# Decoding the second MLP's weights by a clamp in place of a multiplication by a comparison

## The chip, the cores and the metric

The kernel runs on one core of a Trainium2 chip. The metric is the device time of one execution in microseconds (us); a second number, the span, is the time from the first to the last instruction in the profile of one execution.

## The reference

The reference computes causal attention with a window of 64 positions (4 batches, 8 heads, 576 positions, head width 64), and passes its 2304 rows of 512 numbers through two gated MLPs, one after the other:

```python
def _attn_ref(q, k, v):
    ...
    mask = (rel >= 0) & (rel < window)
    ...
    return np.matmul(attn, v).astype(np.float32)

def _moe_ref(x, w_gate, w_val, w_out):
    gate = 1.0 / (1.0 + np.exp(-(x @ w_gate)))
    val = x @ w_val
    return (gate * val @ w_out).astype(np.float32)

def _moe2_ref(x, w_a, w_b, w_out):
    a = x @ w_a
    b = x @ w_b
    return (a * b @ w_out).astype(np.float32)
```

The six weight matrices (512 x 1536, 512 x 1536 and 1536 x 512 for each MLP) reach the kernel as 64-bit floats.

## The kernel before

The kernel computes in pairs: a number is split into a high part, rounded to the format that TensorE multiplies in, and a low part, the rest; three of the four products of such pairs are summed. The hidden width of 1536 is cut into 12 blocks of 128, so each MLP has 12 blocks with three matrices of 128 x 512 numbers each: a and b (into the hidden layer) and o (out of it). Blocks are numbered F = 0 to 11 in the first MLP and 12 to 23 in the second; NF is 12.

Weights arrive as pairs of 32-bit words. A matrix is loaded into a tile `st` (`load_matrix`, L353 for a and b, L351 for o) with the low words at even places and the high words at odd ones (`w0`, `w1`). **Decoding** makes a 32-bit float of it in `decode_words` and `decode_pair`, for each matrix in these steps:

- `low` (L373, ScalarE): the upper three bits of the low word as an integer;
- `ex` (L376, ScalarE): the absolute value of the high word read as a 32-bit float. Its exponent field lies elsewhere than a 64-bit float's, but the value still tells how large the number is;
- `wi` (L379, VectorE): the high word shifted left by 3 and masked; then (L382, VectorE) joined with the sign and the uppermost exponent bit;
- `wi` plus `low` (L386): an integer addition, on GpSimd in the first MLP and on VectorE in the second. In the profile VectorE's form of it bears the name CUSTOM_DVE_ANT_0, and ISA in the order of the program;
- `ex` (L392, VectorE): `ex >= SMALLEST` as 0 or 1, times `wi` read as a float. Numbers too small for the format become zero.

Then the pair is made: the high part on ScalarE (L398), the low part as a subtraction (L401) on VectorE for a and b and on GpSimd for o of the second MLP. The pair is saved (L365) for the later half of the rows. In the second MLP `combining` makes sums and differences of a's and b's halves on GpSimd (L422), their high parts on ScalarE (L427) and low parts on GpSimd (L430): these feed a scheme with 7 products instead of 8 (`quad`), whose products go to the PSUM banks qa, qb and qc (L861), are put together by ScalarE (r, L880) and VectorE (g, qc: L884; qa, qc: L894), and split into the hidden pair hh, hl (L459, L461). The products with o go through `bank_sum` into the sums resf (L1000, added by VectorE in L1004) or through `projection` into xacc (L503, evicted by VectorE in L575). gacc (L528) is the same of the first MLP.

Buffers of the decoding: three tiles `st`, one `low`, two `ex`, one `wi`. An `ex` is kept until the last reader: GpSimd's sums for a and b, GpSimd's subtraction for o.

Order: the first 212 us or so follow a written-out order (`RAMP`). Behind that, Python emits the instructions in the order of the calls (`step_decode` decodes one matrix, `combining` follows b), and the framework's scheduler sets the order on each engine, except where the kernel ties it (`paced`, `held_back`, `in_order`). Each engine then takes its own queue strictly in that order. SyncE (SP) issues the transfers. The decoding of the second MLP begins before the first MLP's last blocks are done and ends at some 534 us; from there on its weights come from memory, decoded.

```python
        (nc.vector if F >= NF else nc.gpsimd).tensor_tensor(out=wi, in0=wi, in1=low, op=ALU.add)
        wordy[F, nm] = ex, wi
```

Of the kernel before, what the change touches and what calls it, by code (L numbers as in the profile page):

```python
# [10 lines left out]
F32 = mybir.dt.float32  # L11
F32R = mybir.dt.float32r
I32 = mybir.dt.int32
U32 = mybir.dt.uint32
AF = mybir.ActivationFunctionType
ALU = mybir.AluOpType
# [5 lines left out]
def tile_window_attention_gated_mlps(ctx, tc, q, k, v, w1g, w1v, w1o, w2a, w2b, w2o, out):  # L22
    nc = tc.nc
    B, H, S, D = q.shape
    NT, DM = out.shape
    DFF = w1g.shape[1]
    P = 128
    NP = H // 2
    NF = DFF // P
# [11 lines left out]
    MASKED = 1.0e30  # L41
    LARGEST = 3.0e38
    SMALLEST = 1.125 * 2.0 ** -15

    keep = lambda name, bufs, **kw: ctx.enter_context(tc.tile_pool(name=name, bufs=bufs, **kw))
    const = keep("const", 1)
# [10 lines left out]
    stage, dec, qp = pool(decoding, "stage", 3), pool(decoding, "dec", 1), pool(early, "qp", 1)  # L57
# [20 lines left out]
    for e in range(2):  # L78
        rows = slice(e * WIN, (e + 1) * WIN)
        nc.gpsimd.affine_select(  # L80
            out=mask_n[rows], in_=mask_n[rows], pattern=[[1, P]], compare_op=ALU.is_ge,
# [3 lines left out]
            out=mask_n[rows], in_=mask_n[rows], pattern=[[-1, P]], compare_op=ALU.is_ge,  # L85
# [218 lines left out]
    staged, parts, ready = {}, {}, {}  # L304
# [59 lines left out]
    def save(F, nm, pair):  # L364
        nc.sync.dma_start(out=kept[F, nm], in_=pair.bitcast(F32))  # L365

    wordy = {}

    def decode_words(F, i, nm):
        st = staged.pop((F, nm))  # L370
        w0, w1 = st[:, :, 0], st[:, :, 1]
        low = dec.tile([P, DM], I32, tag="low", name="low")
        nc.scalar.activation(out=low, in_=w0.bitcast(U32), func=AF.Copy, scale=2.0 ** -29)  # L373
        yield
        ex = dec.tile([P, DM], F32, tag="ex", bufs=2, name="ex")
        nc.scalar.activation(out=ex, in_=w1.bitcast(F32), func=AF.Abs)  # L376
        yield
        wi = dec.tile([P, DM], I32, tag="wi", name="wi")
        nc.vector.tensor_scalar(  # L379
            out=wi, in0=w1, scalar1=3, scalar2=(1 << 30) - 1, op0=ALU.logical_shift_left, op1=ALU.bitwise_and  # L380
        )
        nc.vector.scalar_tensor_tensor(  # L382
            out=wi, in0=w1, scalar=-(1 << 30), in1=wi, op0=ALU.bitwise_and, op1=ALU.bitwise_or
        )
        yield
        (nc.vector if F >= NF else nc.gpsimd).tensor_tensor(out=wi, in0=wi, in1=low, op=ALU.add)  # L386
        wordy[F, nm] = ex, wi
        yield

    def decode_pair(F, i, nm):  # L390
        wf, wi = wordy.pop((F, nm))
        nc.vector.scalar_tensor_tensor(  # L392
            out=wf, in0=wf, scalar=SMALLEST, in1=wi.bitcast(F32), op0=ALU.is_ge, op1=ALU.mult
        )
        yield
        pair = wts.tile([P, 2, DM], F32R, tag=f"w{nm}", name=f"w{nm}")
        wh, wl = pair[:, 0, :], pair[:, 1, :]
        nc.scalar.activation(out=wh, in_=wf, func=AF.Copy)  # L398
        yield
        engine = nc.gpsimd if F >= NF and nm == "o" else nc.vector  # L400
        engine.tensor_tensor(out=wl, in0=wf, in1=wh.bitcast(F32), op=ALU.subtract)  # L401
        parts.setdefault(F, {})[nm] = (wh, wl)
        pairs[F, nm] = pair
        if F >= NF:
            full[F, nm] = wf
        elif nm == "o" and DECODED <= F < 2 * SEVEN:
            nc.sync.dma_start(out=kept_o[F], in_=wf)
        yield
        if F < NF and nm != "o":
            nc.sync.dma_start(out=kept[F, "f"][:, i], in_=wf)  # L410
            yield
# [218 lines left out]
    def begin_matrix():  # L630
        if begun[0] == 0:
            load_weights(DECODED)
        if begun[0] < len(order):
            F, i, nm = m = order[begun[0]]
            begun[0] += 1
            whole(decode_words(*m))
            if F + 1 < NW:
                load_matrix(F + 1, nm)

    def step_decode(turn):  # L640

        if combined_by:
            parts_done[0] += 1
            if next(combined_by[0], combined_by) is combined_by:
                combined_by.pop()
                parts_done[0] = 0
                return True
            if parts_done[0] == 1:
                return True
        if begun[0] == len(order):  # L650
            return False
        F, i, nm = m = order[begun[0]]
        if F > limit[0] or (F > G and last_use.get(F - G - 1, -1) >= turn):
            return False
        begin_matrix()
        whole(decode_pair(*m))
        save(F, nm, pairs.pop((F, nm)))
        if nm == "o":
            ready[F] = parts[F]
        elif nm == "b" and F >= NF:  # L660
            combined_by.append(combining(F))
        return True
# [402 lines left out]
    streams["V"] = call(lambda t=t: load_values(t) for t in range(len(tiles)))  # L1065
    streams["L"] = call(lambda F=F, nm=nm: load_matrix(F, nm) for F, i, nm in order_of)
    streams["D"] = (s for F, i, nm in order_of for s in decode_words(F, i, nm))
    streams["W"] = (s for F, i, nm in order_of for s in decode_pair(F, i, nm))
    streams["K"] = call(lambda F=F, nm=nm: save(F, nm, pairs.pop((F, nm))) for F, i, nm in order_of)
    streams["P"] = call(iter(matmuls))  # L1070
# [122 lines left out]
    for fc in range(NF):  # L1193
        alone = ALONE.get(fc, ())
        for i, f0 in enumerate(alone):
            need(NF + f0, NEVER)
            w = parts[NF + f0]
# [11 lines left out]
        w = parts[NF + fc]  # L1209
# [83 lines left out]
    for n, (ph, fc) in enumerate(steps):  # L1293
# [3 lines left out]
        w = fetched[n]  # L1297
# [118 lines left out]
```

## Time and profile before

| what | value |
|---|---|
| time, median of 3 runs | 945.8 us (945.24 to 946.58) |
| time of the profiled execution | 945.28 us |
| span of the profiled execution | 943.5 us |
| TensorE (PE) busy | 922.2 us, 98% |
| VectorE (DVE) busy | 706.6 us, 75% |
| ScalarE (ACT) busy | 482.2 us, 51% |
| GpSimd (POOL) busy | 306.9 us, 33% |
| TensorE's granted clock, mean | 0.999 of full speed |

An engine's busy time is what its instructions took, not what it worked at its peak. A row of a view names the line of the kernel (L392), the engine, the operation, what is written and read (out<-in, in the program's names) and the shape. "Idle before, <-" tells how long the engine had stood still ahead of the instruction and which instruction's end let it go on.

### The profile page before, as it was taken

The numbers are of one execution on the slowest core, as the hardware profiler recorded it, in microseconds if no ns is written. First come the engines' busy times: TensorE is split into PE (matmuls) and PEld (weight loads), VectorE is DVE, ScalarE is ACT, GpSimd is POOL, SyncE is SP. The second block draws the span as 40 slices with busy tenths as digits, with TensorE's granted clock in tenths as the row PEclk, the third lists the DMA queues.
The fourth block names the chain that finished last, engine by engine and source line by source line (L and its number), as shares of the span: only waits on it lengthen the run. The fifth ranks groups of instructions, "written<-read, shape, count | busy, mean of one in ns | idle before, by whom it ended". The sixth has DMA issues, their size and how long they took to land. (4 is left out here: it accounts for less than half of the span.)

```text
span 943.5 us, 15633 instructions
## 1 busy us (share of the span) xinstructions
PE 922.2 (98%) x5498; PEld 771.9 (82%) x5498; DVE 706.6 (75%) x1370; ACT 482.2 (51%) x1071; POOL 306.9 (33%) x325
## 2 busy tenths in 40 slices
PE   7899999999999999999999999999999999999998
PEld 6798888887888778878787787888888888888886
DVE  6997787786569799898999877687877773354455
ACT  7897555686644456664555446555444233211111
POOL 4543222343226714561655337354351000000000
PEclk9999999999999999999999999999999999999999
DMA  9988598988479626673767758555547675544212
GB/s 225 244 214 239 198 323 290 346 274 250 143 226 315 233 113 200 237 247 142 267 223 250 278 175 234 197 182 168 176 124 240 197 277 147 167 157 146 86 60 89
DMA packets 145566, 195.79 MB, mean 208 GB/s; under 512 B 63569, under 2 KB 98641, under 8 KB 144849
## 3 DMA queue, kind: packets, MB, share of 16 engines
q1 hardware_dynamic: 144400, 192.71, 63.0%
q0 software_dynamic: 1088, 2.10, 1.3%
q8 instruction: 43, 0.70, 0.3%
q14 instruction: 35, 0.28, 0.1%
HBM read 118.75 MB, written 71.57 MB: 202 GB/s over the span
## 5 line engine op out<-in xcount | busy, mean ns | idle before, releaser
L861 PE MATMUL qa<-op,wq 128*128 128x512 f32 x432 | 112.3, 390 | 1.8 <-ACT r L880 1.4
L861 PE MATMUL qb<-op,wq 128*128 128x512 f32 x432 | 111.1, 390 | 0.9 <-POOL wq L430 0.6
L880 ACT ACTIVATE r<-qa 128x512 f32<-128x512 f32 x108 | 62.9, 595 | 95.0 <-PE qa L861 93.4
L450 PE MATMUL gps<-xh,wa 128*128 128x256 f32 (+1 forms) x392 | 104.9, 338 | 1.1 <-DVE g L884 1.1
L450 PE MATMUL vps<-xh,wb 128*128 128x256 f32 (+1 forms) x392 | 105.4, 337 | 0.0
L861 PEld LDWEIGHTS qa<-op,wq 128*128 128x128 f32 x432 | 80.8, 188 | 19.4 <-ACT r L880 2.0
L861 PEld LDWEIGHTS qb<-op,wq 128*128 128x128 f32 x432 | 80.9, 188 | 18.5 <-POOL wq L430 1.0
L551 PE MATMUL accm<-hh,wo 128*128 128x512 f32 (+1 forms) x296 | 85.4, 356 | 1.2 <-DVE gacc L528 1.0
L386 POOL TENSOR_TENSOR wi<-wi,low 128x512 int32<-128x512 int32 x36 | 50.0, 1388 | 112.2 <-DVE wi L382 70.4
L450 PEld LDWEIGHTS gps<-xh,wa 128*128 128x128 f32 x392 | 68.7, 189 | 10.1 <-DVE g L884 1.7
L450 PEld LDWEIGHTS vps<-xh,wb 128*128 128x128 f32 x392 | 68.9, 189 | 7.8 <-issue 0.3
L1000 PE MATMUL accq<-wo,h 128*128 128x512 f32 (+1 forms) x294 | 71.5, 385 | 0.1
L459 ACT ACTIVATE hh<-qa 128x512 fp32r<-128x512 f32 x36 | 21.5, 597 | 91.1 <-DVE qa L894 57.8
L450 PE MATMUL gps<-xl,wa 128*128 128x256 f32 (+1 forms) x196 | 65.6, 335 | 0.6 <-DVE xl L237 0.6
L450 PE MATMUL vps<-xl,wb 128*128 128x256 f32 (+1 forms) x196 | 65.7, 335 | 0.0
L392 DVE SCALAR_TENSOR_TENSOR ex<-ex,wi 128x512 f32<-128x512 f32 x72 | 53.6, 744 | 14.8 <-ACT ex L376 7.0
L1000 PEld LDWEIGHTS accq<-wo,h 128*128 128x128 f32 x294 | 54.5, 188 | 11.3 <-DVE res L1004 0.3
L841 POOL TENSOR_TENSOR wq<-s,wq 128x256 fp32r<-128x256 f32 x48 | 38.4, 865 | 76.2 <-ACT wq L838 76.2
L551 PEld LDWEIGHTS accm<-hh,wo 128*128 128x128 f32 x296 | 52.9, 189 | 11.1 <-DVE gacc L528 3.1
L1000 PE MATMUL accq<-wo,hh 128*128 128x512 f32 x184 | 55.7, 394 | 2.9 <-ACT hh L459 1.9
L189 ACT ACTIVATE pr<-pr,stat 128x128 f32<-128x128 f32 x144 | 54.1, 392 | 7.1 <-DVE stat L183 7.0
L861 PE MATMUL qa<-op,wa 128*128 128x512 f32 x216 | 56.6, 390 | 0.6 <-ACT wb L398 0.6
(187 smaller groups left out, 2178.3 us busy)
## 6 DMA issues: line engine op xcount, KB each, us to landing
wo<-ko SPq DMA_DIRECT2D x27, 512.0 KB, 4.1
wa<-ka SPq DMA_DIRECT2D x27, 512.0 KB, 4.3
st_o<-in_moe_w_out_dram SPq DMA_DIRECT2D x24, 512.0 KB, 4.8
ka<-wa SPq DMA_DIRECT2D x24, 512.0 KB, 5.1
kb<-wb SPq DMA_DIRECT2D x24, 512.0 KB, 4.2
ko<-wo SPq DMA_DIRECT2D x24, 512.0 KB, 5.0
kq<-wq SPq DMA_DIRECT2D x48, 256.0 KB, 4.8
wq<-kq SPq DMA_DIRECT2D x48, 256.0 KB, 3.2
```

What stands on the lines that cost most here:

```text
L189: nc.scalar.activation(out=pr[e][:, j, :], in_=pr[e][:, j, :], func=AF.Exp, bias=nmax[:, e, j:j + 1], scale=-1.0, accum_out=None if t in O ...
L386: (nc.vector if F >= NF else nc.gpsimd).tensor_tensor(out=wi, in0=wi, in1=low, op=ALU.add)
L392: nc.vector.scalar_tensor_tensor(out=wf, in0=wf, scalar=SMALLEST, in1=wi.bitcast(F32), op0=ALU.is_ge, op1=ALU.mult)
L450: nc.tensor.matmul(ps, lhsT=a[:, c * P:(c + 1) * P], rhs=b[:, c, :], start=(n == 0), stop=(n == 3 * NP - 1))
L459: nc.scalar.activation(out=hh, in_=hr, func=AF.Copy, scale=factor)
L551: nc.tensor.matmul(ps[:, m], lhsT=a[:, sl], rhs=b, start=k == 0, stop=k == total - 1)
L841: nc.gpsimd.tensor_tensor(out=t[:, 1], in0=sums[nm], in1=t[:, 0].bitcast(F32), op=ALU.subtract)
L861: nc.tensor.matmul(ps, lhsT=a[:, c * P:(c + 1) * P], rhs=b[:, c, :], start=first and n == 0, stop=n == 5, skip_group_check=True,)
L880: nc.scalar.activation(out=r[n], in_=ps, func=AF.Copy)
L1000: nc.tensor.matmul(ps, lhsT=a, rhs=b, start=n == 0, stop=n == len(pairs) - 1)
```

## The change

The second MLP's matrices (F >= NF) get a decoding of their own, `second_words`. It clamps the absolute value to at least 2^-15, in place (L405 of the changed kernel), shifts and masks that same tile in place (L406) instead of the loaded high words, joins sign and uppermost bit from the loaded words (L409), and adds `low` (L413). A number below 2^-15 has been replaced by 2^-15, whose bits the shift and the mask turn into zero, so no comparison and multiplication follow: `decode_pair` skips that step. What was two tiles `ex` and one `wi` becomes three tiles w0, w1 and w2 of one kind, taken in turn by the second MLP's matrices; the first MLP's use w0 and w1 for `ex` and w2 for `wi`, and do the same steps as before.

```diff
+    LEAST = 2.0 ** -15
...
-    wordy = {}
-
-    def decode_words(F, i, nm):
+    wordy, nword = {}, [0]
+
+    def word(n):
+        nword[0] += 1
+        return dec.tile([P, DM], F32, tag=f"w{nword[0] % n}", name="ex")
+
+    def first_words(F, i, nm):
...
-        ex = dec.tile([P, DM], F32, tag="ex", bufs=2, name="ex")
+        ex = word(2)
...
-        wi = dec.tile([P, DM], I32, tag="wi", name="wi")
+        wi = dec.tile([P, DM], F32, tag="w2", name="wi").bitcast(I32)
...
-        (nc.vector if F >= NF else nc.gpsimd).tensor_tensor(out=wi, in0=wi, in1=low, op=ALU.add)
+        nc.gpsimd.tensor_tensor(out=wi, in0=wi, in1=low, op=ALU.add)
...
+    def second_words(F, i, nm):
...
+        low = dec.tile([P, DM], I32, tag="low", name="low")
+        nc.scalar.activation(out=low, in_=w0.bitcast(U32), func=AF.Copy, scale=2.0 ** -29)
+        yield
+        ex = word(3)
+        nc.scalar.activation(out=ex, in_=w1.bitcast(F32), func=AF.Abs)
+        yield
+        wi = ex.bitcast(I32)
+        nc.vector.tensor_scalar(out=ex, in0=ex, scalar1=LEAST, scalar2=None, op0=ALU.max)
+        nc.vector.tensor_scalar(
+            out=wi, in0=wi, scalar1=3, scalar2=(1 << 30) - 1, op0=ALU.logical_shift_left, op1=ALU.bitwise_and
+        )
+        nc.vector.scalar_tensor_tensor(
+            out=wi, in0=w1, scalar=-(1 << 30), in1=wi, op0=ALU.bitwise_and, op1=ALU.bitwise_or
+        )
+        yield
+        nc.vector.tensor_tensor(out=wi, in0=wi, in1=low, op=ALU.add)
+        wordy[F, nm] = ex
+        yield
+
+    def decode_words(F, i, nm):
+        return (second_words if F >= NF else first_words)(F, i, nm)
+
     def decode_pair(F, i, nm):
-        wf, wi = wordy.pop((F, nm))
-        nc.vector.scalar_tensor_tensor(
-            out=wf, in0=wf, scalar=SMALLEST, in1=wi.bitcast(F32), op0=ALU.is_ge, op1=ALU.mult
-        )
+        wf = wordy.pop((F, nm))
+        if F < NF:
+            wf, wi = wf
+            nc.vector.scalar_tensor_tensor(
+                out=wf, in0=wf, scalar=SMALLEST, in1=wi.bitcast(F32), op0=ALU.is_ge, op1=ALU.mult
+            )
```

The change also sorts the queues anew, from the last part of the first MLP up to the end of the decoding. Two places on VectorE show how. Lines of the changed kernel behind the decoding are 32 higher: its L433 is L401, L607 is L575, L916 is L884, L926 is L894, L1036 is L1004.

The first place lies between a g of one block's scheme and the eviction xacc0 behind it, at some 415 us of the trace of before. On VectorE, before, the last 12 rows down to that eviction:

```order
L379 TENSOR_SCALAR wi_5411<-st_a_5233 128x512
L382 SCALAR_TENSOR_TENSOR wi_5411<-st_a_5233,wi_5411 128x512
L386 ISA wi_5411<-wi_5411,low_5407 128x1024
L392 SCALAR_TENSOR_TENSOR ex_5409<-ex_5409,wi_5411 128x512
L379 TENSOR_SCALAR wi_5432<-st_b_5262 128x512
L382 SCALAR_TENSOR_TENSOR wi_5432<-st_b_5262,wi_5432 128x512
L386 ISA wi_5432<-wi_5432,low_5428 128x1024
L401 TENSOR_TENSOR wa_5418<-ex_5409,wa_5418 128x512
L392 SCALAR_TENSOR_TENSOR ex_5430<-ex_5430,wi_5432 128x512
L379 TENSOR_SCALAR wi_5487<-st_o_5341 128x512
L382 SCALAR_TENSOR_TENSOR wi_5487<-st_o_5341,wi_5487 128x512
L575 TENSOR_TENSOR xacc0_4870<-acc0_5359,xacc0_4870 128x512
```

Ahead of these stand that g (L884) and, behind it, an L386 and an L392 of the matrix before. Now, from g on:

```order
L916 TENSOR_TENSOR g0_5379<-qc_5383,r1_5390 128x512
L409 SCALAR_TENSOR_TENSOR ex_5414<-st_b_5249,ex_5414 128x512
L406 TENSOR_SCALAR ex_5394<-ex_5394 128x512
L409 SCALAR_TENSOR_TENSOR ex_5394<-st_a_5221,ex_5394 128x512
L405 TENSOR_SCALAR ex_5321<-ex_5321 128x512
L406 TENSOR_SCALAR ex_5321<-ex_5321 128x512
L409 SCALAR_TENSOR_TENSOR ex_5321<-st_o_5066,ex_5321 128x512
L413 ISA ex_5321<-ex_5321,low_5319 128x1024
L413 ISA ex_5394<-ex_5394,low_5392 128x1024
L433 TENSOR_TENSOR wa_5402<-ex_5394,wa_5402 128x512
L607 TENSOR_TENSOR xacc0_4864<-acc0_5344,xacc0_4864 128x512
```

Between g and the eviction 13 instructions have become 9; three matrices are under way side by side, in three buffers, where one followed the other.

The second place lies in a later block, at some 520 to 524 us: from behind the second eviction of resf0 to the product qa, which the hidden part hh is made from. On VectorE, before (behind the rows shown comes the last L392 of b):

```order
L379 TENSOR_SCALAR wi_6291<-st_a_6161 128x512
L884 TENSOR_TENSOR qc_6278<-qb_6277,r3_6376 128x512
L382 SCALAR_TENSOR_TENSOR wi_6291<-st_a_6161,wi_6291 128x512
L386 ISA wi_6291<-wi_6291,low_6287 128x1024
L392 SCALAR_TENSOR_TENSOR ex_6289<-ex_6289,wi_6291 128x512
L1004 TENSOR_TENSOR resf1_4826<-accq_6362,resf1_4826 128x512
L379 TENSOR_SCALAR wi_6320<-st_b_6182 128x512
L401 TENSOR_TENSOR wa_6298<-ex_6289,wa_6298 128x512
L382 SCALAR_TENSOR_TENSOR wi_6320<-st_b_6182,wi_6320 128x512
L1004 TENSOR_TENSOR resf1_4826<-accq_6379,resf1_4826 128x512
L386 ISA wi_6320<-wi_6320,low_6316 128x1024
L894 TENSOR_TENSOR qa_6276<-qa_6276,g0_6274 128x512
```

Between the eviction and these stands one more L392. Now:

```order
L409 SCALAR_TENSOR_TENSOR ex_6259<-st_a_6134,ex_6259 128x512
L409 SCALAR_TENSOR_TENSOR ex_6287<-st_b_6154,ex_6287 128x512
L916 TENSOR_TENSOR qc_6248<-qb_6247,r3_6344 128x512
L413 ISA ex_6259<-ex_6259,low_6257 128x1024
L1036 TENSOR_TENSOR resf1_4820<-accq_6330,resf1_4820 128x512
L433 TENSOR_TENSOR wa_6267<-ex_6259,wa_6267 128x512
L413 ISA ex_6287<-ex_6287,low_6285 128x1024
L1036 TENSOR_TENSOR resf1_4820<-accq_6347,resf1_4820 128x512
L926 TENSOR_TENSOR qa_6246<-qa_6246,g0_6244 128x512
```

The clamps and shifts of a and b have moved ahead of the evictions of resf0, and b's word is complete (its L413) in front of qa.

## Rows read from the trace of the kernel before

**Rows 1.** The page: span, busy time of engines, granted clock in 40 slices

```profile
span 943.5 us, 15633 instructions
...
PE 922.2 (98%) x5498; PEld 771.9 (82%) x5498; DVE 706.6 (75%) x1370; ACT 482.2 (51%) x1071; POOL 306.9 (33%) x325
...
PEclk9999999999999999999999999999999999999999
```

**Rows 2.** Busy time by stretches: start:end, length, then each engine's busy us (count)

```profile
core 0: us, PE busy (x) PEld busy (x) DVE busy (x) ACT busy (x) POOL busy (x), PEclk, DMA share, GB/s
...
283.00:354.00 71.00, 68.96 (x330) 55.99 (x329) 60.52 (x85) 33.88 (x65) 37.12 (x39) 1.00 0.61 220
354.00:545.00 191.00, 185.71 (x874) 153.24 (x873) 174.86 (x265) 109.31 (x210) 91.13 (x90) 1.00 0.67 231
...
580.00:920.00 340.00, 340.00 (x1534) 282.64 (x1533) 213.66 (x323) 124.73 (x229) 60.36 (x80) 1.00 0.52 167
```

**Rows 3.** The same view, four stretches of 23.6 us, all matmuls of 512 columns

```profile
448.40:472.00 23.60, 22.26 (x98) 17.87 (x97) 23.16 (x33) 12.63 (x24) 15.13 (x14) 1.00 0.78 267
495.60:519.20 23.60, 22.73 (x100) 18.21 (x99) 23.15 (x36) 13.64 (x26) 13.64 (x14) 1.00 0.76 255
519.20:542.80 23.60, 22.50 (x97) 17.70 (x96) 20.49 (x32) 11.49 (x20) 8.53 (x9) 1.00 0.74 277
613.60:637.20 23.60, 23.60 (x106) 19.52 (x105) 19.73 (x31) 13.37 (x26) 11.68 (x16) 1.00 0.55 179
```

**Rows 4.** TensorE's waits, 283 to 580 us: total us, times, longest

```profile
PE accq L1000 <- ACT hh L459: 1.9, 2, 1.3
PE qa L861 <- ACT r L880: 1.4, 2, 0.9
PE gps L450 <- DVE g L884: 1.1, 1, 1.1
PE accm L551 <- DVE gacc L528: 1.0, 3, 0.5
PE accq L1000 <- DVE xacc L575: 0.9, 2, 0.7
PE qa L861 <- ACT wb L398: 0.6, 1, 0.6
PE qb L861 <- POOL wq L430: 0.6, 1, 0.6
```

**Rows 5.** Timeline at 416 us, DVE and then PE: start, length, instruction [idle before]

```profile
414.42 1.11 DVE L382 SCALAR_TENSOR_TENSOR wi<-st_o,wi 128x512 int32<-128x512 int32 x1
415.45 0.68 DVE L575 TENSOR_TENSOR xacc<-acc,xacc 128x512 f32<-128x512 f32 x1
...
416.19 0.72 PE L1000 MATMUL accq<-wo,hh 128*128 128x512 f32 x2 [0.67 <-DVE xacc L575]
```

**Rows 6.** Groups by line, DVE, 283 to 545 us: count | busy us, mean ns | idle

```profile
L392 DVE SCALAR_TENSOR_TENSOR ex<-ex,wi 128x512 f32<-128x512 f32 x35 | 27.2, 777 | 5.0 <-ACT ex L376 2.3 <-POOL osum L338 0.8 <-POOL wq L430 0.5
...
L379 DVE TENSOR_SCALAR wi<-st_o 128x512 int32<-128x512 int32 x12 | 6.7, 562 | 0.1
L379 DVE TENSOR_SCALAR wi<-st_b 128x512 int32<-128x512 int32 x11 | 6.5, 588 | 0.2
L379 DVE TENSOR_SCALAR wi<-st_a 128x512 int32<-128x512 int32 x11 | 5.6, 507 | 0.1
```

**Rows 7.** Single lines, 283 to 545 us: ns min/median/max, first and last start us

```profile
L392 DVE SCALAR_TENSOR_TENSOR ex<-ex,wi x35: 677/692/1355, 283.7 to 533.4; 128x512 f32<-128x512 f32 x35
...
L379 DVE TENSOR_SCALAR wi<-st_a x11: 410/425/959, 296.0 to 517.3; 128x512 int32<-128x512 int32 x11
L379 DVE TENSOR_SCALAR wi<-st_b x11: 414/426/1401, 302.4 to 521.5; 128x512 int32<-128x512 int32 x11
...
L401 DVE TENSOR_TENSOR wb<-ex,wb x12: 675/1199/1774, 286.5 to 528.1; 128x512 fp32r<-128x512 f32 x12
...
L401 DVE TENSOR_TENSOR wa<-ex,wa x11: 674/687/693, 304.5 to 522.6; 128x512 fp32r<-128x512 f32 x11
```

**Rows 8.** Waits of DVE, then of ACT, 283 to 545 us: total us, times, longest

```profile
DVE ex L392 <- ACT ex L376: 2.3, 3, 1.6
...
ACT ex L376 <- POOL wo L401: 5.7, 4, 1.8
```

More of the change, by code (lines that the diff above doesn't have):

```diff
@@ L385, in decode_words @@
         yield
-        (nc.vector if F >= NF else nc.gpsimd).tensor_tensor(out=wi, in0=wi, in1=low, op=ALU.add)
+        nc.gpsimd.tensor_tensor(out=wi, in0=wi, in1=low, op=ALU.add)
         wordy[F, nm] = ex, wi
         yield
-    def decode_pair(F, i, nm):
-        wf, wi = wordy.pop((F, nm))
-        nc.vector.scalar_tensor_tensor(
-            out=wf, in0=wf, scalar=SMALLEST, in1=wi.bitcast(F32), op0=ALU.is_ge, op1=ALU.mult
-        )
+    def second_words(F, i, nm):
+        st = staged.pop((F, nm))
+        w0, w1 = st[:, :, 0], st[:, :, 1]
+        low = dec.tile([P, DM], I32, tag="low", name="low")
[18 more added lines that the diff above has]
+        return (second_words if F >= NF else first_words)(F, i, nm)
+    def decode_pair(F, i, nm):
+        wf = wordy.pop((F, nm))
[4 more added lines that the diff above has]
+            )
         yield
```

## The prediction

> **What bounds the kernel now.** The page comes first [rows 1]: TensorE is busy for 922.2 of the 943.5 us of the span, at the full clock throughout, so at most some 21 us can be had in all, and VectorE (DVE) stands at 75% on average. An average hides stages, so the table by stretches is next [rows 2]. While the second MLP's weights are decoded (354 to 545 us) DVE is busy for 174.9 of 191 us, 92%, and TensorE stands still for 5.3 us; in the 71 us before, where that decoding begins, TensorE stands still for 2.0 us; from 580 to 920 us TensorE never stands still and DVE has a third of its time free. What the change is worth is decided before 580 us. Third, the table of who made TensorE wait, from 283 to 580 us [rows 4]: DVE is named directly three times (g, gacc, xacc, 3.0 us together), and the evictions on ScalarE (ACT) and the sums on GpSimd (POOL) that are named otherwise mostly wait for a DVE result themselves. The wait at 416.19 us is the pattern [rows 5]: TensorE needs a PSUM bank that the DVE eviction xacc frees; that eviction starts at 415.45 us because a decoding step (L382) ran from 414.42. DVE takes its queue in order, and decoding steps stand in front of the work that TensorE waits for. So this stage is one where a shorter DVE queue should come back, in part, as TensorE time.
>
> **What a stopped TensorE costs.** A wait shows only its idle gap, and refilling costs more. A clean stretch of 23.6 us holds 106 matmuls of 512 columns, 223 ns each; the three that start at 448.4, 495.6 and 519.2 us hold 98, 100 and 97 [rows 3]. The 23 that are missing are worth 5.1 us, while the idle time shown is 1.3, 0.9 and 1.1, together 3.3 us. I count 1.55 us for each us of a gap.
>
> **The change, part by part.** It concerns the 36 matrices of the second MLP, three for each of 12 column blocks.
>
> *The multiplication by a comparison goes* (L392): 36 instructions of the second MLP. In the stretch from 283 to 545 us stand 35 such rows, almost all of them of this MLP; they take 777 ns on average [rows 6], 677 at the least [rows 7].
>
> *A maximum with a constant comes*: 36 instructions, one input and one output of 512 floats, in place. The trace has no such maximum. The nearest row is the shift L379, also a one-input operation with constants on 512 four-byte elements in SBUF: 410 ns at the least, 562, 588 and 507 ns on average for the three matrices [rows 6, 7], so 552 over all. I take that. The lower bound is 410; the upper one is what such a shift takes at the worst of the matrix a, 959 ns [rows 7]. Difference: 36 x (777 - 552) = 8.1 us less DVE time; from 36 x (677 - 410) = 9.6 us less to 36 x (959 - 777) = 6.6 us more.
>
> *Shift, join, integer addition* stay at one each, the shift now reading packed words where it read every other one; 410 ns with the stride leaves no sign that this costs anything, so nothing is counted. ACT and POOL keep their instructions; no transfer is added. The moved loads and stores on SP's queue cost nothing as long as DMA has room: its share is 0.67 in that stretch [rows 2]; without that room a late matrix would be the next thing waited for.
>
> *The buffers* change what waits for what. Before, two result buffers and one word buffer: the third matrix of a block needs the buffer of the first, which POOL frees only after the block's sums, and the next integer word needs the one word buffer. Now three whole buffers rotate, so the first matrix of the next block waits for the sums of this one, and the third for nothing of its own block. The price is that the absolute value by ACT now stands at the head of the DVE chain, where before it was wanted only at its end.
>
> *The order* shows the effect. At the eviction xacc (first place of the order shown) 13 DVE instructions stood between g and xacc, ten of 0.69 us and three of 0.43 [medians in rows 7], 8.2 us; now 9 stand there, six and three, 5.4 us. 2.8 us earlier is more than both waits there, 0.9 us [rows 4]; they go. At the second place, between the second eviction of resf0 and the product qa, ten and two (7.8 us) become eight long ones (5.5 us): the 0.6 us that TensorE waits for the hh made from this qa goes (the smaller one of the two in rows 4). There the word of matrix b is also finished ahead of qa instead of after it, so POOL's sums start earlier and the 0.6 us for wq goes. The same holds one block earlier for the 0.6 us for wb. Of the waits for g (1.1) and gacc (1.0) I count half, since the queue ahead of them shrinks by less than 1 us. The long wait for hh (1.3 us, at 462 us) stays: from the first xacc to qa there the queue holds seven long and one short before (5.3 us) and seven and two now (5.7).
>
> Sum: 0.9 + 0.6 + 0.6 + 0.6 + 0.55 + 0.5 = 3.75 us of gaps, times 1.55 = 5.8 us gained. Against it: that long wait grows by 0.4, and a queue sorted anew will make some new wait, for which I put one of the small ones, 0.6: (0.4 + 0.6) x 1.55 = 1.6 us. Net 4.2 us: the profiled execution goes from 945.28 to 941.1, and since the median shown is 0.5 above that execution, **941.6 us**.
>
> *A rule against it.* Rows first: the subtraction for wa takes 674 to 693 ns, the one for wb, the same form, 1199 at the median [rows 7]; wb's runs while POOL makes its sums. So DVE instructions that read SBUF lengthen beside POOL. The Trainium skill, "SBUF — State Buffer", section "SBUF: two separate sides", says that VectorE and GpSimd share a pair of ports as an exclusive lock, taken by a VectorE operation with two SBUF inputs and also by a one-input one in a two-port mode. By that rule the new maximum fights POOL just as the old multiplication did, and gains only its shorter hold; the sum would keep the 9.6 us of undisturbed times at best, and lose it where POOL is in front. The trace agrees as far as the shift, too, reaches 1401 ns [rows 7].
>
> **The rivals.**
>
> *Contention and reordering eat it (no change).* Of the new maximum, if most fall beside POOL's sums, each takes as much as the old step: the 959 ns against 777 above. Then DVE is as full as before and only the order differs. For it: the shift's maxima [rows 7]. Against it: its medians are within 16 ns of its minimum. Time: the new waits (1.6 us) against the 1 to 2 us that better buffers save, 945 to 946.
>
> *The head of the chain blocks (slower).* DVE reaches the maximum before ACT has made the absolute value, since ACT itself waits for POOL to free the buffer, and everything behind it on DVE, evictions among it, stands. For it: ACT's absolute value waited for POOL 4 times, up to 1.8 us, and DVE for ACT's result 3 times, up to 1.6 us [rows 8]; the new order puts up to three maxima in a row. Against it: with three buffers that release comes earlier. It decides when DVE is held for more per block than it has free, 191 - 174.9 = 16.1 us over the some 9 blocks that 191 us hold (12 blocks in some 250 us, first to last L392 in [rows 7], 21 us each), 1.8 us. If 4 of the 12 blocks lose 1.8 us each in full: 941.6 + 7.2 = 948.8.
>
> *Everything behind DVE goes (much faster).* All idle time from 354 to 545 us, 5.3 us, and half of the 2.0 before: 6.3 x 1.55 = 9.8, so 936.
>
> That the change does something else can be excluded from the order: 36 maxima are there, and no comparison is left behind the twelfth block.
>
> **How the numbers follow.** A measurement of this kernel can tell about 0.2%, 1.9 us, from no change. My forecast (939 to 943.9): 0.54. Much faster (below 939): 0.10. No change (943.9 to 947.7): 0.22. Slower: 0.14. Faster by over 0.2% is then 0.64, within 0.22, slower 0.14. The range from 936.5 to 947 leaves out most of the slower case, a little of the no-change case and half of the much faster one, under 2 in 10.
>
> **What would show it.** DVE's busy time falls from 706.6 to about 698; the maximum near 0.55 us on average; DVE in the decoding stretch below 90%; the waits of TensorE for xacc, wb and wq gone, the one for hh still there; from 580 us on everything the same but earlier. Wrong would be: a maximum of 0.8 us or more; DVE idle in front of the maximum, released by ACT; or TensorE's waits in 283 to 580 us at 8 us as now, under other names.

## The result, and the profile after

| | before | after |
|---|---|---|
| time, median (lowest to highest, runs) | 945.71 us (945.23 to 947.5, 6) | 954.05 us (950.87 to 958.11, 6) |
| ratio, 95% interval | | 1.0085 [1.0064, 1.0106] |
| profiled execution: time, span | 945.28, 943.5 us | 953.24, 951.4 us |

The changed kernel is 8.3 us slower; 941.6 was forecast. The page of after, to be held against [rows 1]:

```profile
span 951.4 us, 15611 instructions
...
PE 921.9 (97%) x5498; PEld 771.3 (81%) x5498; DVE 697.8 (73%) x1370; ACT 480.3 (50%) x1071; POOL 302.3 (32%) x325
```

VectorE did lose 8.8 us of work, and TensorE has as much to do as before, over a longer span. The table of stretches of after (start:end, length, busy us of PE, PEld, DVE, ACT, POOL with counts, granted clock, DMA share, GB/s) answers [rows 2]:

```profile
283.00:354.00 71.00, 66.91 (x319) 54.43 (x317) 54.67 (x82) 31.43 (x62) 41.57 (x44) 1.00 0.63 223
354.00:545.00 191.00, 185.27 (x873) 153.54 (x874) 168.63 (x269) 107.00 (x210) 85.14 (x90) 1.00 0.65 228
...
580.00:920.00 340.00, 336.49 (x1517) 279.33 (x1517) 215.75 (x319) 125.87 (x232) 64.33 (x85) 1.00 0.53 170
```

In the decoding stretch VectorE falls from 174.9 to 168.6 us, 88%, and TensorE gets nothing from it (185.3 against 185.7). The losses lie at both edges: 2 us in 283 to 354, and 3.5 us behind 580, where TensorE never stood still before. The groups of the new steps (count | busy us, mean ns | idle before and releaser), 283 to 545 us, for [rows 6]:

```profile
L413 DVE CUSTOM_DVE_ANT_0 ex<-ex,low 128x1024 uint16<-128x1024 uint16 x34 | 27.3, 803 | 3.1 <-ACT low L399 2.7
...
L406 DVE TENSOR_SCALAR ex<-ex 128x512 int32<-128x512 int32 x34 | 21.5, 633 | 0.4
L405 DVE TENSOR_SCALAR ex<-ex 128x512 f32<-128x512 f32 x34 | 20.6, 605 | 7.2 <-ACT ex L402 6.9
```

The maximum takes 605 ns on average; with the median of 427 in the single lines below (ns min/median/max, first and last start) it lies near the shift in [rows 6, 7], as assumed. Ahead of it VectorE stands idle for 6.9 us until ScalarE's absolute value is made; ahead of the old multiplication that was 2.3 us [rows 8].

```profile
L405 DVE TENSOR_SCALAR ex<-ex x34: 408/427/1334, 286.9 to 525.6; 128x512 f32<-128x512 f32 x34
```

TensorE's waits in after, 283 to 600 us (total us, times, longest), against [rows 4]:

```profile
PE qa L893 <- ACT r L912: 5.4, 3, 3.5
PE accm L583 <- DVE gacc L560: 3.0, 4, 1.7
PE qa L893 <- DVE g L916: 2.1, 1, 2.1
PE qc L893 <- DVE h L493: 1.6, 1, 1.6
PE accq L1032 <- DVE hl L493: 0.7, 1, 0.7
```

With four more of 0.2 to 0.6 they make 14.6 us (11.1 of them up to 580 us); before it was 8.1. xacc, wb and wq are gone, as foretold. In their place stand waits that were not there: for g under qa (at 464 us), for h (at 502), and one of 3.5 us for r at 582, behind the decoding; and the waits for gacc have grown from 1.0 to 3.0 us.

What such a wait looks like shows in the timeline of after at 501 us, DVE and then PE (start, length, instruction [idle before]):

```profile
501.40 1.50 DVE L406 TENSOR_SCALAR ex<-ex 128x512 int32<-128x512 int32 x1
502.82 0.68 DVE L493 SCALAR_TENSOR_TENSOR h<-qc,h 128x512 fp32r<-128x512 f32 x1
...
503.56 1.65 PE L893 MATMUL qc<-op,wa 128*128 128x512 f32 x6 [1.61 <-DVE h L493]
```

It is the pattern of [rows 5], one place further: a decoding step stands in VectorE's queue ahead of the result that TensorE needs. At 464 us the same holds of all four steps of one o, and of one more maximum, ahead of g.

The largest wait. Timeline of after at 577 to 588 us, DVE, then POOL, ACT and PE:

```profile
577.55 1.75 DVE L808 TENSOR_TENSOR op<-xq,op 128x1024 fp32r<-128x1024 f32 x1
579.23 5.44 DVE L808 TENSOR_TENSOR op<-t,op 128x1024 fp32r<-128x1024 f32 x1
584.59 0.68 DVE L916 TENSOR_TENSOR g<-qc,r 128x512 f32<-128x512 f32 x1
...
579.87 3.03 POOL L873 TENSOR_TENSOR wq<-s,wq 128x256 fp32r<-128x256 f32 x4
582.66 0.92 POOL L866 TENSOR_TENSOR s<-wf 128x256 f32<-128x256 f32 x1
...
585.30 0.63 ACT L921 ACTIVATE g<-g 128x512 f32<-128x512 f32 x1 [4.71 <-DVE g L916]
585.84 0.58 ACT L912 ACTIVATE r<-qa 128x512 f32<-128x512 f32 x1
...
586.47 1.66 PE L893 MATMUL qa<-op,wb 128*128 128x512 f32 x6 [3.51 <-ACT r L912]
```

The same place before, DVE, then POOL:

```profile
567.65 5.31 DVE L783 TENSOR_TENSOR t<-xq,t 128x1024 f32<-128x1024 f32 x1
...
574.56 1.74 DVE L776 TENSOR_TENSOR op<-t,op 128x1024 fp32r<-128x1024 f32 x1
576.23 0.68 DVE L884 TENSOR_TENSOR g<-qc,r 128x512 f32<-128x512 f32 x1
...
576.87 3.03 POOL L841 TENSOR_TENSOR wq<-s,wq 128x256 fp32r<-128x256 f32 x4
```

Before, the subtraction that makes the operand (`op<-t,op`) was through at 576.3, ahead of GpSimd's four subtractions; after, it starts 0.6 us before them and takes 5.44 us in place of 1.74. g stands behind it in VectorE's queue, r stands in ScalarE's queue behind a step that waits for g, and TensorE waits for the bank that r frees. Nothing in this place was edited: the second MLP's last decoding ended some 50 us earlier.

### The profile page after: what moved, and what is told of

It reads as the page before. It is cut to its first block, busy times and chain, and to the rows that moved or that the text cites. A ratio compares the mean times of both kernels' runs of the same rounds, so it can differ in the third digit from the quotient of the medians.

```text
span 951.4 us, 15611 instructions
## 1 busy us (share of the span) xinstructions
PE 921.9 (97%) x5498; PEld 771.3 (81%) x5498; DVE 697.8 (73%) x1370; ACT 480.3 (50%) x1071; POOL 302.3 (32%) x325
## 4 chain that ended last, share of the span: by engine, by line
PE 68%; DVE 17%; ACT 5%; POOL 4%; issue 3%; DMA 3%; SPq 0%; POOLq 0%; DVEq 0%; ACTq 0%
PE qa L893 15%; PE accq L1032 10%; PE gps L482 7%; PE vps L482 7%; PE qb L893 7%; PE accm L583 6%; PE qc L893 3%; PE accy L995 3%; DVE ex L409 2%; PE accx L995 2%; DVE ex L413 2%; PE xps L229 2%; DVE ex L405 2%; DVE ex L406 1%; PE sps L171 1%
## 5 line engine op out<-in xcount | busy, mean ns | idle before, releaser
L893 PE MATMUL qa<-op,wb 128*128 128x512 f32 x216 | 55.0, 390 | 3.5 <-ACT r L912 3.5
L893 PE MATMUL qc<-op,wa 128*128 128x512 f32 x216 | 56.2, 390 | 1.6 <-DVE h L493 1.6
```

Source lines behind the costliest of these rows:

```text
L893: nc.tensor.matmul(ps, lhsT=a[:, c * P:(c + 1) * P], rhs=b[:, c, :], start=first and n == 0, stop=n == 5, skip_group_check=True,)
```

## The experiments

The order theory: the new arithmetic saves what was forecast, and the queues, sorted anew by the scheduler, give back more, at a few rows. Against it the arithmetic theory: the new one-input steps are held beside GpSimd, or the clamp at the chain's head waits for ScalarE's absolute value (the rival of the prediction). The port theory: one VectorE operation is held for a GpSimd burst, by chance of timing; the third-buffer theory: decoding that runs further ahead is in the way. Ratios are to executions of before that were timed beside each run, with 95% intervals.

**a1_again.** The changed kernel, not edited.

> The changed kernel itself once more, unedited, for a second trace. Order theory (the queues that the scheduler sorted anew put decoding and weight-sum work ahead of what TensorE waits for): the TensorE waits at 342, 466, 504 and 586 us are all there again, within 0.5 us each, and the median is 951 to 956 us. Port theory (a VectorE operation is held for as long as a GpSimd burst lasts, by chance of their timing): the waits at 342, 466 and 504 us are there, but the operand subtraction near 579 us that took 5.44 us is between 1.2 and 5.5 us, and the time of the run goes with it: a run without it is about 3.7 us shorter, 949.5 us.

953.98 us, 1.0069 [1.0049, 1.0090], with the same waits in its trace (r 5.4, 3, 3.5; gacc 3.0; g 2.0; h 2.1), and the subtraction takes 5.43 us again. The loss is fixed to places and comes again; it is no matter of chance between executions.

**e5_order_dve_pe** and **e6_order_dve.** The changed kernel with VectorE's queue from some 300 us in the order of before, the new steps in the places of the old ones; in e5 TensorE's queue too. A helper ties each instruction of an engine to the one before it:

```diff
+    def given_order(engine, ranks):
+        made = [i for i in nc.cur_bb.bb.instructions if i.engine == engine]
+        for a, b in zip(ranks, ranks[1:]):
+            tc.add_manual_dep(made[b], made[a].name, ...)
+    given_order(mybir.EngineType.DVE, [...])
+    given_order(mybir.EngineType.PE, [...])
```

> The new arithmetic with VectorE's and TensorE's queues in the order that they had before the change (the clamp in the shift's place, the shift in the join's, the join in the addition's, the addition in the comparison's), from about 300 us on. Order theory: the saving of VectorE (8 to 9 us) comes through as forecast and the time is 941 to 944 us. Arithmetic theory (the new one-input operations are held by GpSimd bursts, or the clamp waits for ScalarE at the head of the queue): it stays at 949 to 954 us, with the same long waits under qa and qc.

> As the run before it, with VectorE's queue alone in the old order; TensorE's is the scheduler's. Order theory with VectorE as the place: 941 to 946 us, at most 2 us behind the run with both. If TensorE's own order is what costs, it stays above 949 us while the run with both is below 945.

e5: 954.02, 1.0078 [1.0059, 1.0098]; e6: 955.14, 1.0088 [1.0065, 1.0112]. TensorE's waits in e5, 235 to 600 us:

```profile
PE accm L583 <- ACT hh L491: 6.5, 2, 6.2
PE accq L1032 <- DVE xacc L607: 4.4, 2, 4.2
...
PE qa L893 <- ACT r L912: 1.4, 2, 1.0
```

By the number alone this speaks for the arithmetic theory; by the places it doesn't. The wait of 3.5 us for r is gone (1.0 at the most), as are those of 2.1 for g and 1.6 for h under qa and qc; instead one of 6.2 us stands at 273 us, at the edge of the tied stretch, and one of 4.2 at 422. ScalarE's and GpSimd's queues, sorted freely around the one held, don't fit it: ahead of the maximum VectorE stands 16.1 us for ScalarE, in 283 to 545 us,

```profile
L405 DVE TENSOR_SCALAR ex<-ex 128x512 f32<-128x512 f32 x34 | 18.2, 536 | 16.1 <-ACT ex L402 16.1
```

against 6.9 in after. Inconclusive on the sum. e5 and e6 are not told apart, so TensorE's own order is not what costs here.

**e3_two_words.** Two word buffers in place of three.

```diff
-        ex = word(3)
+        ex = word(2)
```

> The new arithmetic with two buffers for the decoded words in place of three, so that the scheduler sorts a third way. Order theory: the time is as arbitrary as its order, anywhere from 943 to 956 us, and its TensorE waits stand at other places than the changed kernel's. Third-buffer theory (decoding that runs further ahead is what gets in the way): 941 to 945 us. Arithmetic theory: 950 to 955 us.

955.17, 1.0081 [1.0054, 1.0109]: not told apart from after, so the third-buffer theory falls. The order theory had expected other places; the tail is the same, with a subtraction of 5.43 us at 578.52. The two theories left are not told apart by this run.

**bt_control, f2t_old_queues, f1t_three_old_queues.** VectorE, TensorE and ScalarE tied in one order for all three. bt has the old arithmetic, its shift, join, addition and multiplication together at the place of the old multiplication; f2t and f1t have the new four steps there, with two word buffers and with three.

From f2t to f1t:

```diff
-        ex = word(2)
+        ex = word(3)
```

> The control for the run before it: the old arithmetic with the same fixing of the queues (shift, join, addition and comparison of a matrix together where the comparison stood). Order theory: 944 to 948 us, near the kernel before, and 3 to 8 us above the run with the new arithmetic in the same queues. Arithmetic theory: the same 944 to 948 us, but below the run with the new arithmetic. If both are far above 948 us, standing the four together is itself what costs, and only the difference of the two tells anything.

> The new arithmetic alone, in the queues of before: two buffers for the words as before the change (any free one is taken), TensorE's queue exactly as before, VectorE's and ScalarE's as before except that the clamp, shift, join and addition of a matrix stand together where the comparison stood. Order theory (the forecast's sums were right and the newly sorted queues ate them): 939 to 944 us, and the TensorE waits at 342, 466, 504 and 586 us that the changed kernel has are gone. Arithmetic theory (the new operations are held by GpSimd, or wait for ScalarE at the head of the queue): 947 to 954 us.

> As the first run of these, with the third word buffer of the change. Order theory: as that run, 938 to 944 us, a little less where ScalarE can run further ahead. Third-buffer theory (more buffers let the loads and ScalarE's copies run into what TensorE needs): 3 us or more above it.

bt: 957.25, 1.0133 [1.0114, 1.0153]. f2t: 959.94, 1.0158 [1.0142, 1.0173]. f1t: 951.22, 1.0063 [1.0046, 1.0080]. All three lie outside what either theory expected: the order alone costs 12 us (bt), so only differences tell. The group of the maximum, 235 to 560 us, in f2t and then in f1t:

```profile
L407 DVE TENSOR_SCALAR ex<-ex 128x512 f32<-128x512 f32 x36 | 19.2, 535 | 10.0 <-ACT ex L404 9.0 <-POOL osum L339 0.8
```

```profile
L407 DVE TENSOR_SCALAR ex<-ex 128x512 f32<-128x512 f32 x36 | 19.6, 543 | 2.5 <-ACT ex L404 2.3
```

The head's wait is real: with two buffers in one order VectorE stands 9.0 us for ScalarE, with three 2.3, and the third buffer is worth 8.7 us there. The change brings the third buffer along. Against bt in the same order, the new arithmetic takes 2.7 us more with two buffers and 6.0 us less with three.

**n1_swapped_copies.** The kernel before, in which only two ScalarE operations of the second decoding that don't depend on each other (`low`, `ex`) are written in the other sequence.

```diff
-        low = ...; nc.scalar.activation(out=low, ...)
         ex = ...;  nc.scalar.activation(out=ex, ...)
+        low = ...; nc.scalar.activation(out=low, ...)
```

> The kernel before with nothing but two independent ScalarE operations of the second MLP's decoding written in the other order (the absolute value ahead of the low word's copy), so that the scheduler sorts the queues anew with the same work in them. Order theory: the time moves by more than 2 us from 945.7 us, most likely up (948 to 955 us), without any change of the work. Arithmetic theory: 945 to 947 us, since nothing was changed that costs.

949.07, 1.0040 [1.0025, 1.0055]: 4.2 us slower (before beside it: 944.9) with the arithmetic untouched. Its trace keeps step with before to within 0.8 us until 563 us and loses 3.2 us by 586, at the place of after. DVE, then PE:

```profile
569.46 0.42 DVE L466 SCALAR_TENSOR_TENSOR hl<-vps,hh 128x256 fp32r<-128x256 f32 x1 [1.92 <-ACT hh L464]
569.80 5.32 DVE L781 TENSOR_TENSOR op<-t,op 128x1024 fp32r<-128x1024 f32 x1
...
578.38 0.68 DVE L889 TENSOR_TENSOR g<-qc,r 128x512 f32<-128x512 f32 x1
...
580.91 2.82 PE L866 MATMUL qa<-op,wb 128*128 128x512 f32 x6 [2.27 <-ACT r L885]
```

The held subtraction is no longer than the one that before has (5.31 us), but it starts 2.15 us later (569.80 against 567.65), since ScalarE makes hh later, and g comes 2.15 us later (578.38 against 576.23). So this tail is fragile with the old arithmetic already, and the arithmetic theory is not needed for it. What does the new sorting disturb there? In ScalarE's queue at 556 to 578 us some 19 rows stand otherwise in after: bank copies (`added`, L1034) that wait for TensorE's accq are ahead of the copies (L807) that VectorE's operands are made from. Timeline of after, ACT:

```profile
561.22 0.60 ACT L1034 ACTIVATE added<-accq 128x512 f32<-128x512 f32 x1 [1.00 <-PE accq L1032]
561.71 1.05 ACT L807 ACTIVATE op<-t 128x1024 fp32r<-128x1024 f32 x1
```

**x1_tail** (after, those rows in the order of before), **b1_reverse_tail** (before, those rows in the order of after), **x2_dve_moves** (after, six VectorE results moved ahead of decoding steps or sums: gacc at 307 and 341 us, qa and g at 464, h at 502, hl at 529) and **x12_both**. From here on all queues are tied to their own order but for the rows named. ScalarE in x1 and VectorE in x2 against after:

```diff
 L506 ACTIVATE hr<-gps
-L1034 ACTIVATE added<-accq
 L807 ACTIVATE op<-t
 L491 ACTIVATE hh<-vps
...
+L1034 ACTIVATE added<-accq
+L807 ACTIVATE op<-t
+L491 ACTIVATE hh<-vps
 L1034 ACTIVATE added<-accq
 L870 ACTIVATE wq<-s x4
-L807 ACTIVATE op<-t
-L491 ACTIVATE hh<-vps
```

```diff
 L405 TENSOR_SCALAR ex<-ex
+L926 TENSOR_TENSOR qa<-qa,g
 L406 TENSOR_SCALAR ex<-ex
+L916 TENSOR_TENSOR g<-qb,r
 L409 SCALAR_TENSOR_TENSOR ex<-st_o,ex
 L413 ISA ex<-ex,low
-L926 TENSOR_TENSOR qa<-qa,g
 L405 TENSOR_SCALAR ex<-ex
-L916 TENSOR_TENSOR g<-qb,r
```

> The changed kernel with every queue fixed in its own order, except some 20 rows of ScalarE between 556 and 578 us, which take the order of before: the operand copies and hidden copies ahead of the bank copies that wait for TensorE. No work differs. Order theory: the TensorE waits at 577 and 582 to 586 us (1.4 and 3.5 us) shrink to the one of 0.9 us that the kernel before has, and the time falls by 4 to 5 us, to 949 to 950 us. Port theory (the 5.4 us subtraction is held by GpSimd whenever it runs, whatever ScalarE does): the wait stays, 953 to 954 us.

> The kernel before, old arithmetic, every queue fixed in its own order, except the same some 20 rows of ScalarE at 552 to 575 us, which take the order that the changed kernel has. Order theory: 948 to 951 us, 3 to 6 us above the kernel before, with one operand subtraction of over 5 us in the way of the sum that TensorE waits for. If the new arithmetic has to be there for that wait to come about, 945 to 946 us.

> The changed kernel with every queue fixed in its own order, except that on VectorE six operations that TensorE waits for stand some places earlier, ahead of decoding and weight sums: one accumulator eviction at 307 and one at 341 us, the products of sum and gate at 464 us (two), the hidden remainder at 502 us and one at 529 us. Order theory: the waits of 1.7, 2.1, 1.6 and 0.65 us there go or shrink to under 0.5 us each, and the time falls by 3 to 6 us, to 948 to 951 us. If what is late there is not the queue but the operand (ScalarE, TensorE itself), it falls by less than 1 us.

> Both edits of the two runs before it. Order theory: the gains add, 942 to 946 us, at or under the kernel before: what the change costs is then all in some 30 rows of two queues. If something else in the new work costs, it stays above 949 us.

| kernel | us | ratio |
|---|---|---|
| x1_tail | 950.01 | 1.0040 [1.0028, 1.0052] |
| b1_reverse_tail | 950.51 | 1.0047 [1.0030, 1.0063] |
| x2_dve_moves | 952.5 | 1.0070 [1.0052, 1.0088] |
| x12_both | 947.27 | 1.0011 [1.0001, 1.0021] |

The rows of ScalarE at the tail take 4.0 us off after's 954.05, and put 4.7 us on the 945.8 of before timed beside them. Timeline of b1, DVE, then POOL:

```profile
576.46 4.06 DVE L776 TENSOR_TENSOR op<-t,op 128x1024 fp32r<-128x1024 f32 x1
580.45 0.68 DVE L884 TENSOR_TENSOR g<-qc,r 128x512 f32<-128x512 f32 x1
...
577.11 2.33 POOL L841 TENSOR_TENSOR wq<-s,wq 128x256 fp32r<-128x256 f32 x3
```

and of x1, DVE, then POOL:

```profile
573.30 5.00 DVE L815 TENSOR_TENSOR t<-xq,t 128x1024 f32<-128x1024 f32 x1
...
579.90 1.74 DVE L808 TENSOR_TENSOR op<-t,op 128x1024 fp32r<-128x1024 f32 x1
581.57 0.68 DVE L916 TENSOR_TENSOR g<-qc,r 128x512 f32<-128x512 f32 x1
...
573.23 3.29 POOL L873 TENSOR_TENSOR wq<-s,wq 128x256 fp32r<-128x256 f32 x4
576.02 1.19 POOL L866 TENSOR_TENSOR s<-wf 128x256 f32<-128x256 f32 x1
```

In both directions the same rows decide which subtraction is held: in x1 another one (`t`), with time to spare, and g starts 3.0 us sooner than in after. x2 alone is not told apart from after, and misses its 948 to 951: its waits for g under qa and for h go, but the longest ones for hh and op, both made by ScalarE, grow from 0.6 to 1.6 and 1.3 us. On top of x1 the six moves take 2.7 us. x12 stays above the 942 to 946 that the order theory put, so more than these rows is in it.

**x3_more_moves, x4_last_moves; b2_before_moves, b3_before_last_moves.** The same treatment carried on: rows that a wait of TensorE names are moved ahead of decoding steps, 8 in x3 on top of x12, 9 more in x4; and on the kernel before with its old arithmetic 6 in b2 (g, xacc twice, qa twice, hh) and 4 in b3. One move of x4 and one of b2:

```diff
 L916 TENSOR_TENSOR g<-qc,r
 L406 TENSOR_SCALAR ex<-ex
+L1036 TENSOR_TENSOR resf<-accq,resf
 L405 TENSOR_SCALAR ex<-ex
...
-L1036 TENSOR_TENSOR resf<-accq,resf
```

```diff
 L392 SCALAR_TENSOR_TENSOR ex<-ex,wi
-L379 TENSOR_SCALAR wi<-st_o
-L382 SCALAR_TENSOR_TENSOR wi<-st_o,wi
 L575 TENSOR_TENSOR xacc<-acc,xacc
+L379 TENSOR_SCALAR wi<-st_o
+L382 SCALAR_TENSOR_TENSOR wi<-st_o,wi
```

> The run with both edits, and eight more rows moved ahead of decoding and weight sums where its trace still shows TensorE waiting: on VectorE the second eviction at 308 us and one at 341 us, the products and the hidden remainder at 422 and 464 us, an output sum at 502 us; on ScalarE the hidden copy at 422 and 464 us. Saving theory (the arithmetic saves what was forecast, and only the order of the queues eats it): 942 to 945 us, below the kernel before. Slack theory (what VectorE saves is not on TensorE's path in well ordered queues either): 945 to 947 us, no better than the run with both edits.

> The kernel before, old arithmetic, with every queue fixed in its own order and six rows moved in the same way (VectorE: a sum at 381 us, two output sums at 415 us, the product at 461 and 523 us; ScalarE: the hidden copy at 461 us), ahead of decoding. Saving theory: 942 to 944 us by the waits of 1.1, 0.9, 1.3 and 0.5 us that go, but not below the changed kernel with its moves by more than 1 us. Slack theory: as low as the changed kernel with all its moves or lower, since the order of the queues is what sets the time and the arithmetic is hidden: 941 to 943 us.

> The run with the further moves, and nine more rows moved where its trace still shows TensorE waiting: on VectorE the gate's product and the hidden remainder at 309 us, an operand difference at 341 us, output sums at 482 and 501 us; on ScalarE the hidden copy at 309 us and the sums' copies at 463, 480 and 574 us. Saving theory: 941 to 943 us, clearly under the kernel before and within 2 us of the forecast. Slack theory: 944 us as the run before it, new waits in place of the old ones.

> The old arithmetic with its moves and four more (VectorE: the product at 382 us, an output sum at 415 us, addition and comparison of a matrix at 507 us). Saving theory: 943.5 to 945 us, at least 1 us above the changed kernel with all of its moves, since VectorE has no room left between 354 and 545 us (174.9 of 191 us busy). Slack theory: 942 to 943 us, as low as the changed kernel.

| kernel | us | ratio |
|---|---|---|
| x3_more_moves | 944.26 | 0.9993 [0.9982, 1.0003] |
| x4_last_moves | 942.66 | 0.9966 [0.9953, 0.9979] |
| b2_before_moves | 944.94 | 0.9998 [0.9989, 1.0007] |
| b3_before_last_moves | 945.84 | 1.0002 [0.9992, 1.0012] |

The stretch 354 to 545 us in x4, then in b3:

```profile
354.00:545.00 191.00, 190.09 (x896) 157.62 (x895) 165.24 (x269) 107.15 (x210) 84.84 (x90) 1.00 0.66 237
```

```profile
354.00:545.00 191.00, 186.28 (x869) 152.96 (x869) 175.17 (x265) 108.34 (x209) 90.87 (x90) 1.00 0.67 232
```

VectorE's maximum in x4, 283 to 545 us:

```profile
L405 DVE TENSOR_SCALAR ex<-ex 128x512 f32<-128x512 f32 x34 | 20.5, 603 | 7.6 <-ACT ex L402 7.2
```

In x4 TensorE stands still for 0.9 of 191 us while VectorE is busy for 165.2; with the old arithmetic VectorE stays at 175.2, and the moves win nothing that can be measured. TensorE's waits of x4, 283 to 600 us, sum to 5.6 us with the largest of 1.7. VectorE's idle time before the maximum, released by ScalarE, is 7.2 us in x4 and 6.9 in after: with that wait in place x4 computes the same with the same operations as after, and beats both kernels, by its ratio 3.2 us under before (2.7 by the medians). So the head's wait is not what makes after slow. b2 gains less than either theory had put.

## Why the prediction was wrong

**Right: what VectorE saves.** 8.1 us were forecast, 8.8 came. The maximum takes 605 ns where 552 was put, and the shift, 633, got longer too; the addition (857 ns before, 803 now) and the join (30.7 us in all from 283 to 545 us before, 26.9 now), to which nothing was done, got shorter. The sum came out right partly by luck.

**Right: what that saving can be worth.** 4.2 us net were forecast. With the queues put right it is 3.2 (x4), and the ten moves on the old arithmetic (b2, b3) gave 0 ± 0.1%: the gain belongs to the change and not to the moves alone, as far as those ten show. x4 has 23 moves and the 19 rows of the tail; that as many on the old arithmetic would win nothing isn't shown. The waits for xacc, wb and wq that the order was read for went. That 3.2 lies near 4.2 is in part luck: x4 got there by rows placed by hand, not by the waits that the sum counted.

**Wrong: "a queue sorted anew will make some new wait, for which I put one of the small ones, 0.6".** That is the failed step. From before to after TensorE's waits grew from 8.1 to 14.6 us, although those for xacc, wb and wq, 2.1 us, went. Matmul by matmul, after and a1_again fall 2.3 to 2.6 us behind before between 283 and 349 us, stand at 545 us within 1 us of where they stood at 354, and lose 4.3 and 5.8 us from 563 to 586. The term that stood at 0.6 x 1.55 = 0.9 us measured at about 4 us at the tail alone (x1, b1), and some 2.7 us at the six VectorE rows (x12 against x1). Two terms of the sum went with it: gacc, counted as half gone, rose from 1.0 to 3.0 us, and at 462 us, where hh's long wait was to grow by 0.4, TensorE waits 2.1 us for g instead. In the profiled execution 1.1 us more are lost at 24 to 31 us, in a1_again, the same kernel, nothing there: that part differs between executions.

Of the signs of being wrong two came: VectorE idle in front of the maximum for ScalarE (6.9 us), which by x4 is not the cause, and TensorE's waits, 11.1 us up to 580 us under other names, which are part of it. And from 580 us on things were not "the same but earlier".

**Why it was sized so.** The order was read for VectorE, at two places of the decoding. ScalarE's queue, where the rows at 556 to 578 us stood otherwise, was not read, and "from 580 us on everything the same but earlier" was taken for granted. Some 270 of ScalarE's 950 rows in the program stand at another place in after, and some 330 of VectorE's 1226. A comparison of the queues on the engines that TensorE waits for, up to its next long clean stretch, would have shown the bank copies ahead of the operand copy; that a subtraction would then be held for 5 us, only the row at 567.65 us of before hinted at.

**The rivals.** The head of the chain (slower) gave the right sign at 948.8, some 3 us up where 8.3 came, but not the cause: its wait is there (6.9 us in after, 9.0 in f2t, 16.1 in e5) and depends on the order and the buffers, yet x4 has it too and is faster than before. "Contention and reordering eat it" had the mechanism and forecast no change, since it, too, sized the new waits by 1.6 us. The rule against the forecast was weighed for the clamp, where it mattered little (605 ns); where VectorE was held long was an operand subtraction that no edit touched.

**1.55 us for each us of a gap.** Within one execution it is not one price. Matmul by matmul, from 235 to 600 us, the profiled execution of after falls 6.5 us behind before with 6.5 us more of gaps, 1.0 each; a1_again falls 8.8 us behind with 5.7 more, 1.5 each, and there the granted clock was 0.50 behind two of the stops (rows below). x4 gains 3.5 us with 2.5 less, 1.4 each, without such a difference of the clock: why stays open.

## What to carry to other kernels

When a scheduler sorts the queues, an edit buys what it saves plus a new throw of the order: here 4 us (0.4%) came from swapping two independent copies, and 4 us from some 19 rows that the edit did not touch, as much as the edit's worth or more. Read the order of every engine that the bound engine waits for, up to the end of the disturbed stretch and not only where the edit lies; and judge an arithmetic change with the rows on the wait path put right in both kernels. Where a result feeds the bound engine, look at its place in its queue first: six rows moved forward were worth 2.7 us here.

## What the runs showed of the hardware

A VectorE subtraction of 128 x 1024 with both inputs in SBUF takes 1.22 us while GpSimd stands still, as here in before:

```profile
558.14 1.22 DVE L783 TENSOR_TENSOR t<-xq,t 128x1024 f32<-128x1024 f32 x1
```

It took 5.44 us in after, 5.31 in before, 5.00 in x1 and 4.06 in b1, where three or four of GpSimd's subtractions ran beside it (2.33 to 3.29 us together), with a sum right behind them except in b1. It was not slowed in proportion: it ended 1.08 to 1.09 us behind the end of the last of these in all four (in after 579.23 + 5.44 against 582.66 + 0.92, in x1 573.30 + 5.00 against 576.02 + 1.19, in b1 576.46 + 4.06 against 577.11 + 2.33), nearly its own undisturbed length, as if it began only then. (In n1 the 5.32 us ended 1.70 us behind the last sum, 572.51 + 0.91, and GpSimd issued a transfer in between: how close the end follows isn't fixed.) The Trainium skill, "SBUF — State Buffer", section "SBUF: two separate sides", says that the shared pair of ports is an exclusive lock for a whole instruction, which fits; that a whole run of separate instructions can keep it from VectorE is what these rows add.

The granted clock after a stop differs between executions of one kernel. In a1_again, behind the stop of 3.5 us before 586 us, the stretch from 586 to 589 has a granted clock of 0.50, the lower level of 1.2 GHz, and so has 504 to 507, behind the waits at 502; windows (all engines, then PE) and timeline:

```profile
504.00:507.00 3.00, 3.00 (x9) 2.35 (x8) 2.52 (x5) 0.69 (x2) 0.00 (x0) 0.50 0.94 333
...
582.00:586.00 4.00, 0.49 (x3) 0.97 0.96 228
586.00:589.00 3.00, 3.00 (x7) 0.50 0.28 98
```

```profile
585.92 2.93 PE L893 MATMUL qa<-op,wb 128*128 128x512 f32 x6 [3.51 <-ACT r L912]
```

In after, behind the same stop, the clock stays at 1.00 (2.4 GHz) and the six matmuls take 1.66 us:

```profile
586.00:589.00 3.00, 2.53 (x11) 1.00 0.44 156
```

So a long stop costs 1.3 us more in some executions. The mean granted clock bears this out over the whole kernel: 0.9973 over the six executions of after and 0.9958 over the five of a1_again, against 0.9996 over the eight of before timed beside a1_again. A share of 0.0023 to 0.0038 less of some 950 us would be 2 to 4 of the 7 to 8 us lost, by my estimate from these clocks. That this is also why after spreads over 7.2 us and before over 2.3 is argued, not shown.
